# Opening of a fused attention and ReGLU kernel: scores of two tiles moved between the sums of the last image pair, half of that pair's last lines summed on TensorE

## Chip, cores, metric

One core of a Trainium2 chip (trn2). The metric is the device time of one execution in microseconds (us); lower is better. Times are compared only within the same rounds.

## The reference, cut to what matters

```
kv_pool = mean of kv over 4 x 4 pixels          # kv [4, 384, 32, 128] -> 768 keys per image
k = v   = kv_pool @ w_sr
a       = softmax(q @ k.T / sqrt(128))          # q [4, 12288, 128]
x       = a @ v
out     = (relu(x @ w_gate) * (x @ w_val)) @ w_out      # d_ff 1536; 49152 rows
```

## The kernel before

The rows of q are worked in 96 tiles of 512. The 768 keys of an image are six chunks of 128, loaded and pooled as three **pairs** of chunks (0, 1, 2). A pair arrives as four **lines** (the four pixel rows that are averaged), one transfer of 512 KB each. Its pooling is a sum of sixteen parts. In the opening most of that sum is done on TensorE: 128 x 128 transposes that accumulate in one PSUM bank turn and add at once. VectorE first adds two lines, which halves the number of transposes.

Only the opening, before the loop reaches its steady state, is touched by the change. Its helpers:

```python
def turn_add(b, pair, lines, first=False, final=False, chunks=(0, 1)):
    n = lines.shape[2]
    for h in chunks:
        for i in range(n):                                     # n = 4
            nc.tensor.matmul(kv_Ts[b, pair][:, h], lines[:, h, i], ident, is_transpose=True,
                start=(first and h == i == 0), stop=(final and i == n - 1), skip_group_check=True)
    if final and h == 1:
        kvT = work.tile([128, 2, 128], FP32, tag="kvT", bufs=2)
        nc.vector.tensor_copy(kvT, kv_Ts[b, pair])             # "the copy"
        kv_Ts[b, pair] = kvT

def project(b, pair):                                          # matmul with w_sr, then scaling on VectorE
    ...
def scores(k, jc):                                             # one 512-column matmul, one exponential
    s_ps = bank([128, T])
    nc.tensor.matmul(s_ps, kv16[:, k // NST, jc, 0:C], qT_of(k), start=True, stop=True)
    nc.scalar.activation(aTs[k][:, jc, :], s_ps, AF.Exp, scale=qk_scale)

def attend(k, pair):                                           # eight value matmuls
    for jc in (2 * pair, 2 * pair + 1):
        for half in range(2):
            values(k, jc, half)

def add_lines(pair, dh, engine, chunks=slice(0, 2)):           # line dh + line dh + 1
    ...
    engine.tensor_tensor(s2[:, chunks], line(pair, dh)[:, chunks], line(pair, dh + 1)[:, chunks], op=ALU.add)
    return s2
```

The part of the opening that the change touches:

```python
turn_open(0, 1)
turn_add(0, 1, add_lines(1, 0, nc.vector), first=True)
attend(0, 0)
for h in range(2):
    s2 = add_lines(1, 2, nc.vector, slice(h, h + 1))
    turn_add(0, 1, s2, final=True, chunks=[h])
attend(1, 0)
add_lines(2, 0, nc.gpsimd, slice(0, 1))
s2 = add_lines(2, 0, nc.vector, slice(1, 2))
...                                                            # weights and q loads issued from GpSimd
project(0, 1)
for k in range(GRP):                                           # GRP = 4
    for jc in range(2, 4):
        scores(k, jc)
    if k == 0:
        turn_values(0, 1)
    if k == 1:
        turn_open(0, 2)
        turn_add(0, 2, s2, first=True)
        for h in range(2):
            s2 = add_lines(2, 2, nc.vector, slice(h, h + 1))
            turn_add(0, 2, s2, final=True, chunks=[h])
    if k == 2:
        project(0, 2)
attend(0, 1)
attend(1, 1)
for jc in range(4, NJC):                                       # NJC = 6
    scores(0, jc)
turn_values(0, 2)
for jc in range(4, NJC):
    scores(1, jc)
attend(0, 2)
...                                                            # reciprocals, values kept, turned; scores of tiles 2, 3
```

The bank pool has eight PSUM banks. In the traces each engine's instructions start in the order written (below, for example, an addition of VectorE at 20.66 us that waited for a transfer, and behind it a scaling at 21.27).

The softmax here doesn't subtract the row's maximum and nothing guards it: scores larger than these inputs give would overflow.

## Time and profile before

| | before |
|---|---|
| time, median of the first 3 runs | 1048.71 us (1048.25 to 1049.2) |
| span of the profiled run | 1046.4 us |
| TensorE idle in its matmul records, 24 to 33 us | 1.29 us |
| TensorE waits, 43 to 1043 us | none |

The lines that carry the argument are shown in the prediction. Four moments, each the start of an instruction, are used throughout the rest:

- **a1**: VectorE starts to add lines 2 and 3 of pair 1, because the last of them has landed.
- **t0**: the first score matmul of pair 1 (tile 0) starts.
- **a2**: VectorE starts to add lines 2 and 3 of the last pair, because the last of them has landed.
- **V**: the first value projection, with which the loop begins.

In the order of time of the kernel before (start, length, engine, line of the program, operation, tiles, count, idle time just before and what ended it), a1, t0, a2 and V are these four:

```profile
17.42 1.29 DVE L343 TENSOR_TENSOR kv_s<-parts 128x512 f32<-128x512 f32 x2 [0.44 <-DMA parts<-in_kv_dram]
...
21.33 0.60 PE L185 MATMUL bank_ps<-qT,kv 128*128 128x512 f16 x2 [0.52 <-DVE kv L167]
...
24.00 1.29 DVE L343 TENSOR_TENSOR kv_s<-parts 128x512 f32<-128x512 f32 x2 [1.62 <-DMA parts<-in_kv_dram]
...
32.82 0.38 PE L234 MATMUL bank_ps<-xT,wv 128*128 128x512 f16 x1
```

Each of the two additions waited for a transfer. V lies 8.82 us behind a2.

### The profile page before, as it was taken

How to read it: one execution, taken by the hardware profiler on the slowest of the kernel's cores; microseconds unless marked ns; L12 is line 12 of the kernel's file. 1: busy time of each engine (PE TensorE's matmuls, PEld its weight loads, DVE VectorE, ACT ScalarE, POOL GpSimd, SP SyncE). 2: the span in 40 equal slices, each digit the busy share in tenths (PEclk: the TensorE clock that was granted, in tenths of full speed). 3: DMA queues.
4: the chain of work that ended last, by engine and by line, in shares of the span. 5: the costliest groups of instructions: out<-in, count | busy, mean ns of one | idle time of the engine just before them, and what ended most of it. 6: DMA issues, size and time to landing. Idle time of an engine off the chain costs nothing.

```text
span 1046.4 us, 25971 instructions
## 1 busy us (share of the span) xinstructions
PE 1036.4 (99%) x9980; PEld 691.1 (66%) x9980; DVE 913.8 (87%) x1680; ACT 908.5 (87%) x1741; POOL 107.6 (10%) x127
## 2 busy tenths in 40 slices
PE   7999999999999999999999999999999999999998
PEld 6566666666666666666666666666666666666665
DVE  3788889898888888898888888889988888888898
ACT  2988888888888888888888888888888888888887
POOL 2000045200000015500000003430000000000000
PEclk9999999999999999999999999999999999999999
DMA  8833256231322335523224134551331322212111
GB/s 302 119 81 69 70 191 162 57 87 32 84 54 62 76 122 140 154 62 72 54 64 87 31 87 132 147 152 40 78 65 53 72 63 55 67 32 67 32 47 47
DMA packets 125853, 90.75 MB, mean 87 GB/s; under 512 B 103328, under 2 KB 104224, under 8 KB 125728
## 3 DMA queue, kind: packets, MB, share of 16 engines
q1 hardware_dynamic: 120288, 75.85, 26.8%
q0 software_dynamic: 5440, 13.24, 7.7%
q8 instruction: 78, 1.28, 0.5%
q14 instruction: 47, 0.39, 0.1%
HBM read 52.76 MB, written 25.17 MB: 74 GB/s over the span
## 4 chain that ended last, share of the span: by engine, by line
PE 97%; DMA 2%; SPq 0%; DVE 0%; ACT 0%; issue 0%; DVEq 0%; ACTq 0%
PE bank_ps L255 25%; PE bank_ps L234 24%; PE bank_ps L245 24%; PE bank_ps L196 12%; PE bank_ps L185 12%; DMA parts<-in_kv_dram 1%; DMA q<-in_q_dram 1%; PE bank_ps L166 0%; PE bank_ps L154 0%; SPq L128 0%; ACT val L238 0%; PE bank_ps L174 0%; PE bank_ps L227 0%; DVE kv_s L343 0%; DVE rinv L204 0%
## 5 line engine op out<-in xcount | busy, mean ns | idle before, releaser
L248 DVE SCALAR_TENSOR_TENSOR hT<-bank_ps,val 128x512 f16<-128x512 f32 x1152 | 759.6, 686 | 100.9 <-ACT val L238 74.5
L238 ACT CAST val<-bank_ps 128x512 f16<-128x512 f32 x1152 | 677.8, 591 | 112.1 <-PE bank_ps L234 107.5
L255 PEld LDWEIGHTS <-hT 128*128 128x128 f16 x4608 | 351.4, 98 | 199.9 <-issue 0.4
L255 PE MATMUL bank_ps<-wo,hT 128*128 128x128 f16 x4608 | 443.2, 219 | 0.0
L234 PE MATMUL bank_ps<-xT,wv 128*128 128x512 f16 x1152 | 436.6, 379 | 0.1
L245 PE MATMUL bank_ps<-xT,wg 128*128 128x512 f16 x1152 | 435.7, 378 | 0.1
L186 ACT ACTIVATE aT<-bank_ps 128x512 f16<-128x512 f32 x576 | 346.3, 605 | 18.4 <-PE bank_ps L185 18.4
L196 PE MATMUL bank_ps<-kv,aT 128*128 128x129 f16 x2304 | 223.3, 219 | 0.0
L196 PEld LDWEIGHTS <-aT 128*128 128x128 f16 x2304 | 177.3, 98 | 68.4 <-issue 0.4
L185 PE MATMUL bank_ps<-qT,kv 128*128 128x512 f16 x576 | 216.4, 379 | 1.5 <-DVE kv L167 0.8
L245 PEld LDWEIGHTS <-wg 128*128 128x128 f16 x1152 | 111.5, 97 | 66.1 <-issue 1.0
L234 PEld LDWEIGHTS <-wv 128*128 128x128 f16 x1152 | 112.7, 98 | 0.4 <-issue 0.4
L212 DVE TENSOR_TENSOR x<-bank_ps,rinv 128x256 f16<-128x256 f32 x188 | 79.7, 424 | 6.7 <-DVE rinv L204 0.2
L78 POOL DMA_DIRECT2D q<-in_q_dram x23 | 12.5, 543 | 571.8 <-DMA qT<-q 571.5
L273 DVE TENSOR_SCALAR o_sb<-bank_ps 128x512 f32<-128x512 f32 (+1 forms) x95 | 64.0, 673 | 1.3 <-PE bank_ps L255 1.3
L137 POOL TENSOR_TENSOR s<-parts 128x512 f32<-128x512 f32 x36 | 45.3, 1270 | 162.7 <-DMA parts<-in_kv_dram 122.3
L185 PEld LDWEIGHTS <-kv 128*128 128x128 f16 x576 | 55.9, 98 | 2.4 <-DVE kv L167 1.4
L204 DVE RECIPROCAL rinv<-bank_ps 128x2 f32<-128x2 f32 x192 | 30.5, 159 | 1.2 <-PE bank_ps L196 1.2
L139 POOL TENSOR_TENSOR s<-s 128x512 f32<-128x512 f32 x18 | 22.8, 1268 | 1.4
L141 POOL TENSOR_TENSOR c<-s 128x256 f32<-128x256 f32 x18 | 13.0, 725 | 1.4
L161 DVE COPY kvT<-bank_ps 128x256 f32<-128x256 f32 x12 | 5.0, 415 | 7.2 <-PE bank_ps L154 7.2
L154 PE MATMUL bank_ps<-ident,kv_s 128*128 128x128 f32 x50 | 7.8, 275 | 1.6 <-DVE kv_s L343 1.6
(37 smaller groups left out, 83.3 us busy)
## 6 DMA issues: line engine op xcount, KB each, us to landing
parts<-in_kv_dram SPq DMA_DIRECT2D x48, 512.0 KB, 6.1
out_dram<-o_sb SPq DMA_DIRECT2D x95, 256.0 KB, 2.1
q<-in_q_dram POOLq DMA_DIRECT2D x23, 512.0 KB, 5.2
xT<-x SPq DMA_TRANSPOSE x94, 2.5
q<-in_q_dram SPq DMA_DIRECT2D x1, 768.0 KB, 7.9
wv<-in_moe_w_val_dram POOLq DMA_DIRECT2D x2, 192.0 KB, 4.6
wg<-in_moe_w_gate_dram POOLq DMA_DIRECT2D x2, 192.0 KB, 5.1
wo<-in_moe_w_out_dram POOLq DMA_DIRECT2D x1, 384.0 KB, 9.9
```

The lines of the kernel that those rows point to most:

```text
L137: eng.tensor_tensor(s2[:, i], parts[:, 2 * i, h], parts[:, 2 * i + 1, h], op=ALU.add)
L185: nc.tensor.matmul(s_ps, kv16[:, k // NST, jc, 0:C], qT_of(k), start=True, stop=True)
L186: nc.scalar.activation(aTs[k][:, jc, :], s_ps, AF.Exp, scale=qk_scale)
L196: nc.tensor.matmul(x_ps[:, i, :], aTs[k][:, jc, s * 128 : (s + 1) * 128], kv16[:, k // NST, jc, C : 2 * C + 1], start=(jc == 0 and i == 0) ...
L204: nc.vector.reciprocal(rinvs[k, half], x_banks[k, half][:, :, C : C + 1])
L212: nc.vector.tensor_tensor(x16s[k][:, 2 * half : 2 * half + 2, :], x_ps[:, :, 0:C], rinv.to_broadcast([128, 2, C]), op=ALU.mult,)
L234: nc.tensor.matmul(va_ps, wv16[:, fb * 128 : (fb + 1) * 128], xTs[k], start=True, stop=True)
L238: nc.scalar.copy(val, va_ps)
L245: nc.tensor.matmul(g_ps, wg16[:, fb * 128 : (fb + 1) * 128], xTs[k], start=True, stop=True)
L248: nc.vector.scalar_tensor_tensor(hTs[k][:, fb, :], g_ps, 0.0, vals.pop((k, fb)), op0=ALU.max, op1=ALU.mult)
L255: nc.tensor.matmul(o_ps, hTs[k][:, fb, s * 128 : (s + 1) * 128], wo16[:, fb, :], start=first, stop=(fb == NFB - 1), skip_group_check=True,)
L273: nc.vector.tensor_scalar(o_sb, o_ps, 1.0 / X_SCALE**2, None, op0=ALU.mult)
```

## The change

The intent: fill the time in which TensorE and ScalarE wait for the last pair's last line with the scores of tiles 2 and 3 for pair 1, and shorten the path from that line to the copy. For this, chunk 0 of lines 2 and 3 is turned straight from the landed lines (eight transposes) while VectorE adds chunk 1 alone (four transposes). The value matmuls of tile 1 for pair 1 also move, from in front of the last pair's first scores to behind them.

```diff
--- before.py
+++ after.py
@@ -382,36 +382,35 @@
     nc.gpsimd.dma_start(wo16, moe_w_out.rearrange("(fb f) c -> f fb c", f=128))
     q_load(2)
     project(0, 1)
-    for k in range(GRP):
-        for jc in range(2, 4):
+
+    def scores_of(k, pair):
+        for jc in (2 * pair, 2 * pair + 1):
             scores(k, jc)
-        if k == 0:
-            turn_values(0, 1)
-        if k == 1:
-            turn_open(0, 2)
-            turn_add(0, 2, s2, first=True)
-            for h in range(2):
-                s2 = add_lines(2, 2, nc.vector, slice(h, h + 1))
-                turn_add(0, 2, s2, final=True, chunks=[h])
-        if k == 2:
-            project(0, 2)
+
+    scores_of(0, 1)
+    turn_values(0, 1)
+    scores_of(1, 1)
+    turn_open(0, 2)
+    turn_add(0, 2, s2, first=True)
+    scores_of(2, 1)
+    turn_add(0, 2, line(2, 2), chunks=[0])
+    turn_add(0, 2, line(2, 3), chunks=[0], final=True)
+    turn_add(0, 2, add_lines(2, 2, nc.vector, slice(1, 2)), chunks=[1], final=True)
+    scores_of(3, 1)
+    project(0, 2)
     attend(0, 1)
+    scores_of(0, 2)
+    turn_values(0, 2)
+    scores_of(1, 2)
     attend(1, 1)
-    for jc in range(4, NJC):
-        scores(0, jc)
-    turn_values(0, 2)
-    for jc in range(4, NJC):
-        scores(1, jc)
     attend(0, 2)
     for half in range(2):
         keep_sums(0, half)
     for half in range(2):
         keep_values(0, half)
-    for jc in range(4, NJC):
-        scores(2, jc)
+    scores_of(2, 2)
     x_turn_pe(0)
-    for jc in range(4, NJC):
-        scores(3, jc)
+    scores_of(3, 2)
     attend(1, 2)
     for half in range(2):
         keep_sums(1, half)
```

## The prediction

> **What bounds the kernel now.** I write S(k,p) for the two score matmuls of query tile k with pooled-image pair p (pairs 0 to 2, so pair 1 is the second and pair 2 the last), E(k,p) for the two exponentials on ScalarE that follow, and A(k,p) for the eight value matmuls that use those. I read the page first, then the waits of TensorE by stage, then the chain of waits and the order of time over the opening.
>
> The page: busy shares, the slices, and the chain that ended last.
>
> ```profile
> PE 1036.4 (99%) x9980; PEld 691.1 (66%) x9980; DVE 913.8 (87%) x1680; ACT 908.5 (87%) x1741; POOL 107.6 (10%) x127
> PE   7999999999999999999999999999999999999998
> PE 97%; DMA 2%; SPq 0%; DVE 0%; ACT 0%; issue 0%; DVEq 0%; ACTq 0%
> ```
>
> The reader is to see one engine that never stops after the first slice. Asked for TensorE's waits from 43 to 1043 us, the profile lists none. Every slot of that stretch is filled by matmuls in program order, so whatever brings the start of that stretch forward by x us should bring the end forward by x, and nothing else in the change touches it. The whole question lies before 43 us. The busy time by stage (first column TensorE) shows how much room there is:
>
> ```profile
> 24.00:33.00 9.00, 7.71 (x69) 4.99 (x70) 4.33 (x13) 6.28 (x12) 2.13 (x4) 1.00 1.22 180
> 33.00:42.50 9.50, 8.96 (x74) 5.25 (x73) 7.54 (x18) 7.66 (x19) 0.53 (x1) 1.00 0.88 125
> ```
>
> TensorE is idle by these records for 1.29 us in the first stage and 0.54 us in the second. The chain of waits for that stage, in order of time (start, length, what):
>
> ```profile
> 12.22 11.65 DMA parts<-in_kv_dram
> ...
> 24.00 0.70 DVE kv_s L343
> ...
> 24.75 1.27 PE bank_ps L154 x8
> ...
> 26.04 0.44 DVE kvT L161
> ...
> 26.61 0.67 PE bank_ps L166 x2
> ...
> 27.71 0.91 PE bank_ps L196 x16
> ...
> 30.34 0.28 DVE rinv L204 x2
> 30.62 0.36 DVE x L212
> ```
>
> The last line of the last pair lands at 23.87. Until VectorE has added lines 2 and 3, TensorE has nothing to do, although S(2,1) needs only what has been there since 21.3. ScalarE waits with it. From the order of time:
>
> ```profile
> 22.62 1.03 PE L154 MATMUL bank_ps<-ident,kv_s 128*128 128x128 f32 x8
> 24.75 1.26 PE L154 MATMUL bank_ps<-ident,kv_s 128*128 128x128 f32 x8 [1.10 <-DVE kv_s L343]
> 25.84 0.59 PE L185 MATMUL bank_ps<-qT,kv 128*128 128x512 f16 x2
> 26.25 1.08 ACT L186 ACTIVATE aT<-bank_ps 128x512 f16<-128x512 f32 x2 [2.44 <-PE bank_ps L185]
> ```
>
> 1.10 us of TensorE and 2.44 us of ScalarE are lost in that one hole.
>
> **What the Trainium skill says.** "Perfetto Trace Analysis", § Identifying the Most-Contended Engine: a high matmul busy share does not say how near the engine is to its roofline. Here 99% against 66% for weight loads. I therefore rest on the empty list of waits and the in-order chain, not on the 99%. "VectorE: DVE Perf Modes", § The TRN2 errata: an fp32 addition of two tensors takes (N+151)/0.96 ns, so 691 ns for N=512. The trace agrees (0.69 us each, two in 1.29). "TensorE: Matmul & The Clock Gate", § Part 4: PE-mode transpose: some 275 ns in one kernel. The trace agrees in length (272 to 273), but what counts here is the spacing: eight in 1.03 us, so (1.03-0.27)/7 = 0.108 us. "PSUM — Partial Sum Buffer", § Specifications: 8 banks. In this stage four hold the running sums of tiles 0 and 1 and one the open transposes, so three are left for scores, and a score can wait for an exponential; the built program shows such waits.
>
> **The change part by part.** The order of instructions in the built program shows: S(2,1) before the sums of lines 2 and 3; chunk 0 of lines 2 and 3 as eight transposes straight from the landed lines, with four from a VectorE sum for chunk 1; S(3,1) before the projection; A(1,1) after S(1,2). Removed: one addition of 0.69 us. Added: four transposes, 4 x 0.108 = 0.43 us on TensorE. From the first value projection on, both programs have the same order, with waits that differ only in the first projection. The count of banks used is the same.
>
> I carry TensorE's clock through. The steps taken from the trace: 0.22 us per 512-column matmul, 0.057 per value matmul (16 in 0.91), exponential 0.41 after its score starts, one each 0.515, each ending after 0.61; transposed pair copy to projection 0.57 (26.04 to 26.61); projection to its scaling 0.71; scaling to score 0.49 (20.84 to 21.33); projection occupies TensorE 0.51.
>
> - The eight early transposes end issue at 22.62 + 8 x 0.108 = 23.49. S(2,1) starts there instead of at 25.84, since its banks were freed by exponentials of 22.27 and 22.78. TensorE is free at 23.92. E(2,1) starts at 23.90, no longer at 26.25.
> - Eight transposes of chunk 0, 23.92 to 24.79. Line 3 is there at 23.87; four of line 2 stand before it. Chunk 1's addition, 24.00 to 24.69, lies beside them. Its four transposes issue 24.79 to 25.22, the last ends at 25.11 + 0.27 = 25.39. The copy starts at 25.42, against 26.04: **0.62 us earlier**.
> - S(3,1) fills 25.22 to 25.66. Projection 25.42 + 0.57 = 25.99, scaling 26.70, A(0,1) from 26.50 to 26.96 beside it. S(0,2) at 26.70 + 0.49 = 27.19, against 28.46: **1.27 us earlier**, because before S(3,1), A(0,1) and A(1,1) all stood in front of it although its keys were ready (27.32 + 0.49 = 27.81).
> - Some is given back. S(0,2) 27.19 and 27.41, two transposes, S(1,2) first at 27.74. Its second waits for a bank until the exponential of 27.60 ends, 28.25. Then A(1,1), 8 x 0.057 = 0.46, 28.47 to 28.93. A(0,2) follows without a wait; before, its second half waited for an exponential until 30.04. Six of its eight are issued at 28.93 to 29.22, ending 29.43, so the reciprocal starts at 29.45, against 30.34: **0.89 us earlier**.
> - From there the chain is the old one. First turned values 31.03 - 0.89 = 30.14, S(3,2) 30.59, first value projection 32.82 - 0.89 = 31.93. ScalarE: its last four exponentials start at 29.8, 30.3, 31.0 and 31.5, the last ends at 32.1, before the first value cast at 32.34.
>
> Sum: **0.89 us**. Time 1048.71 - 0.89 = **1047.8 us**.
>
> **The rivals.**
> 1. **Only the sums count.** If the larger step at S(0,2) were wholly paid back by A(1,1) and the bank wait, the gain would be the 0.62 us of the earlier copy or less: 1048.1. For: between S(1,2)'s two halves TensorE has only three free banks. Against: 28.46 was set by order, and A(0,2)'s old wait disappears.
> 2. **A transfer anchors the start of the steady stage.** The next four query tiles are loaded and turned by transfers whose times do not move; the turn is done at 39.8 at the latest (the next load, which waits for it, starts at 39.81). They are first read at 42.33, afterwards 41.4, so 1.6 us are left. The output weights are issued at 24.52 and land 9.9 us later, 34.4, first used at 41.24. Neither binds. If one did, the gain would shrink to nothing: 1048.7.
> 3. **The coupled stage 33 to 42 takes the gain.** There VectorE and ScalarE wait in turns for each other (three ScalarE waits for reciprocals of 0.46 to 0.57). But both are fed by the value projections and should shift with them. If the shift let TensorE run ahead and wait longer at the end, the gain would be 0.3 to 0.6: 1048.2.
> 4. **Direct transposes are slower.** Those of pair 0, straight from lines, took 421 ns in the median, with weight loads of 231 against 140. If this came from the source and not from a TensorE just out of idleness, eight at 0.18 add 0.58 us to that step and eat the 0.62: 1048.4 or so. For the other reading: weight loads of the same identity were slow too.
>
> **Range and chances.** The three runs of before spread by 0.95 us, as much as the gain. The chain's uncertainty is some 0.4 each way, a median of few runs adds 0.4, and the landing at 23.87 can itself move by some tenths. So 1046.9 to 1048.9 for 8 in 10. 2% would be 21 us, and the opening before 43 us has 1.8 us of TensorE idle after 24 us in all: within 2% is all but certain, 0.99.
>
> **What would show it.** In the profile after: the 1.10 us hole at 24.75 gone and E(2,1) at about 23.9; the twelve transposes 23.9 to 25.4; the copy at 25.4; S(0,2) at 27.2; a bank wait of some 0.3 us in S(1,2); the first reciprocal at 29.45; the first value projection at 31.9; the first matmul with output weights near 40.35; and after 42 us no wait of TensorE, the same distance to the end. It would be wrong if the pair landed later for reasons of its own, if direct transposes were spaced at 0.18 us, or if TensorE began to wait in the stage from 33 to 42.

## The result, and the profile after

The changed kernel took 1047.75 us in the median of six runs (1047.64 to 1048.29); before took 1048.48 us in the six runs of the same rounds and the first look (1047.68 to 1049.20). Ratios in this document are the mean time of one kernel's runs over the mean of the other's runs of the same rounds, so they are not quite the ratio of the medians: here 0.9995, with a 95% interval of 0.9982 to 1.0007. The interval is wide against the effect, so most of the evidence below comes from moments inside the traces, which repeat to some hundredths of a us.

The page of the changed kernel, the lines that answer to those of before:

```profile
PE 1036.3 (99%) x9984; PEld 691.0 (66%) x9984; DVE 913.6 (87%) x1679; ACT 908.6 (87%) x1741; POOL 107.6 (10%) x127
PE   8999999999999999999999999999999999999998
PE 97%; DMA 1%; SPq 1%; DVE 1%; ACT 0%; issue 0%; DVEq 0%; ACTq 0%
```

Four matmuls more, one VectorE instruction less, as the diff says; the first slice went from 7 to 8 tenths. The opening in the order of time:

```profile
18.04 1.29 DVE L343 TENSOR_TENSOR kv_s<-parts 128x512 f32<-128x512 f32 x2 [1.09 <-DMA parts<-in_kv_dram]
...
21.84 0.60 PE L185 MATMUL bank_ps<-qT,kv 128*128 128x512 f16 x2 [0.52 <-DVE kv L167]
...
22.27 3.24 ACT L186 ACTIVATE aT<-bank_ps 128x512 f16<-128x512 f32 x6 [3.79 <-PE bank_ps L185]
...
24.00 0.59 PE L185 MATMUL bank_ps<-qT,kv 128*128 128x512 f16 x2
24.06 0.69 DVE L343 TENSOR_TENSOR kv_s<-parts 128x512 f32<-128x512 f32 x1 [1.18 <-DMA parts<-in_kv_dram]
...
24.43 1.04 PE L154 MATMUL bank_ps<-ident,parts 128*128 128x128 f32 x8
...
32.46 0.38 PE L234 MATMUL bank_ps<-xT,wv 128*128 128x512 f16 x1
```

The reader is to see two things. First, the hole is gone: TensorE goes from the two scores at 24.00 into the direct transposes at 24.43 without a wait, and ScalarE's six exponentials stand in one block. Second, this run did not start as the run of before did: a1 is 18.04 and not 17.42, t0 21.84 and not 21.33, while a2 hardly moved (24.06 against 24.00). Pair 1's last line landed 0.6 us later in that run, although the two kernels are the same up to there. Measured from its own t0, V comes after 10.62 us, against 11.49 before. Measured against the clock it comes only 0.36 us earlier, and the span is 0.3 us shorter.

The chain of waits says the same. Before it ran back from the loop to the last line's transfer. After it does not pass that line at all, but runs back through the work of pair 1 to pair 1's last line:

```profile
7.02 10.92 DMA parts<-in_kv_dram
...
18.04 0.70 DVE kv_s L343
...
24.59 1.33 PE bank_ps L154 x12
```

### The profile page after: what moved, and what is told of

Same layout as the page of the kernel before. It is cut to its first block, busy times and chain, and to the rows that moved or that the text cites. A ratio compares the mean times of both kernels' runs of the same rounds, so it can differ in the third digit from the quotient of the medians. Undisturbed runs are those within 1.5% of the kernel's fastest.

```text
span 1046.1 us, 25977 instructions
## 1 busy us (share of the span) xinstructions
PE 1036.3 (99%) x9984; PEld 691.0 (66%) x9984; DVE 913.6 (87%) x1679; ACT 908.6 (87%) x1741; POOL 107.6 (10%) x127
## 4 chain that ended last, share of the span: by engine, by line
PE 97%; DMA 1%; SPq 1%; DVE 1%; ACT 0%; issue 0%; DVEq 0%; ACTq 0%
PE bank_ps L255 25%; PE bank_ps L234 24%; PE bank_ps L245 24%; PE bank_ps L196 12%; PE bank_ps L185 12%; DMA parts<-in_kv_dram 1%; PE bank_ps L154 1%; PE bank_ps L166 1%; SPq L128 0%; ACT aT L186 0%; ACT x L210 0%; ACT val L238 0%; SPq L93 0%; PE bank_ps L174 0%; DVE hT L248 0%
## 5 line engine op out<-in xcount | busy, mean ns | idle before, releaser
L144 POOL TENSOR_TENSOR kv_s<-c 128x128 f32<-128x128 f32 x18 | 8.2, 454 | 1.4
```

## The experiments

The theory after this reading: the opening has **two starts that compete**. One is the last line's landing (a2), the other is the work of pair 1 in front of it (t0, which is a1 + 3.8: 3.91 in the profile of before, 3.80 in that of after). Before, V was set by a2 and came at a2 + 8.82. After, V is set by t0 and comes at t0 + 10.62. So the gain is (a2 + 8.82) - (t0 + 10.62): 0.87 us with the landings of the profile of before, 0.42 with those of the profile of after. The main rival is the simple reading of the change: a hole of 1.1 us was filled with scores, and that is the gain, wherever the landings fall. All kernels below gave correct results.

### Only the new order

Lines 2 and 3 of both chunks are again added on VectorE; the order of scores and values is the new one.

```diff
-    turn_add(0, 2, line(2, 2), chunks=[0])
-    turn_add(0, 2, line(2, 3), chunks=[0], final=True)
-    turn_add(0, 2, add_lines(2, 2, nc.vector, slice(1, 2)), chunks=[1], final=True)
+    for h in range(2):
+        s2 = add_lines(2, 2, nc.vector, slice(h, h + 1))
+        turn_add(0, 2, s2, final=True, chunks=[h])
```

> The new order of scores and values is kept, but both chunks of lines 2 and 3 are again added on VectorE. Let t0 be the start of the first score matmul of pair 1, a2 the start of VectorE's addition of the last pair's lines, V the first value projection. Before: V = a2 + 8.82 in its profile. After: V = t0 + 10.62 in its profile. Theory (last line's landing and the work of pair 1 are two competing starts, and the direct lines are worth more than the order): the copy of the turned pair comes at a2 + 2.04 as before, and V = the later of a2 + 8.56 and t0 + 10.62; so only 0.26 us earlier than before for the same a2. Rival (the gain comes from the scores pulled into the hole): V 0.5 to 0.9 earlier than a2 + 8.82.

a2 was 23.89. The copy and V, in the order of time of this kernel:

```profile
25.93 0.42 DVE L161 COPY kvT<-bank_ps 128x256 f32<-128x256 f32 x1 [0.75 <-PE bank_ps L154]
...
32.45 0.38 PE L234 MATMUL bank_ps<-xT,wv 128*128 128x512 f16 x1
```

The copy is at a2 + 2.04, V at a2 + 8.56, exactly as the theory had it: the new order as a whole is worth 0.26 us against the same landing, not 0.5 to 0.9. (Two parts are in it, the scores in the hole and the moved values of tile 1; the run "The values of tile 1 put back" parts them.) The time shows nothing (mean 1048.26, before 1048.13 in the same rounds, ratio 1.0001, 0.9988 to 1.0013).

### Only the lines on TensorE

The order of before, with the direct transposes of chunk 0.

```diff
-            for h in range(2):
-                s2 = add_lines(2, 2, nc.vector, slice(h, h + 1))
-                turn_add(0, 2, s2, final=True, chunks=[h])
+            turn_add(0, 2, line(2, 2), chunks=[0])
+            turn_add(0, 2, line(2, 3), chunks=[0], final=True)
+            turn_add(0, 2, add_lines(2, 2, nc.vector, slice(1, 2)), chunks=[1], final=True)
```

> The old order of scores and values, but chunk 0 of lines 2 and 3 straight on TensorE. Theory: copy at a2 + 1.38 when the landing is late, and V = the later of a2 + 8.16 and t0 + 10.44, so 0.66 us earlier than before for the same a2, and in some draws of the two landings even earlier than the full change. Rival (the gain comes from the scores pulled into the hole): V at a2 + 8.6 or later, no more than 0.2 us earlier than before. Time of the run 1047.8 against 1048.2 to 1048.5.

Measured, in the order of time of this kernel:

```profile
22.07 0.60 PE L185 MATMUL bank_ps<-qT,kv 128*128 128x512 f16 x2 [0.52 <-DVE kv L167]
...
32.52 0.38 PE L234 MATMUL bank_ps<-xT,wv 128*128 128x512 f16 x1
```

The landings were a1 = 18.26 and a2 = 23.75, so t0 was late and the last line early. V is t0 + 10.45; the theory gave 10.44. The rival's moment (a2 + 8.6 or later) is met too, with a2 + 8.77, because the last line came early; so this run supports the bound by t0 but does not tell the two readings apart. The full change would have had V at t0 + 10.62 = 32.69 in this draw: here a part of the change is better than the whole. The next run shows which part of the rest costs these 0.17 us. The worth of the direct lines for a late landing (0.66 us by the steps) was not reached in this draw; the run with the values cut in two, below, shows it at the copy. The mean was 1047.95, before 1048.13 in the same rounds (ratio 0.9997, 0.9984 to 1.0011).

### The values of tile 1 put back

```diff
     attend(0, 1)
+    attend(1, 1)
     scores_of(0, 2)
     turn_values(0, 2)
     scores_of(1, 2)
-    attend(1, 1)
```

> The full change, but the value matmuls of tile 1 for pair 1 stand again in front of the scores of tile 0 for the last pair. My prediction counted their move as part of the order's gain (the scores come 0.22 us earlier). Theory from the trace of after: the first score of the last pair comes 0.22 us later against the copy (1.99 in place of 1.76), but the reciprocal comes 1.88 after that score and not 2.28, so V is 0.17 us earlier than after for the same start: the later of t0 + 10.45 and a2 + 7.73. Rival (the move is a gain): V 0.2 us or more later than t0 + 10.62.

t0 was 21.93 and V 32.38, so V came at t0 + 10.45: 0.17 us earlier than with the full change, as the theory had it. The move of the eight value matmuls brings the last pair's scores forward by 0.22 us, but 0.46 us of values then stand between those scores and the first reciprocal, and only part of it fills a wait. This part of the change is a small loss. The scores themselves are neutral in such a draw: the run before, without them in the hole, had the same t0 + 10.45. (Mean 1047.81, before 1048.13, ratio 0.9997, 0.9984 to 1.0009.)

### Pair 1 treated in the same way

```diff
-    for h in range(2):
-        s2 = add_lines(1, 2, nc.vector, slice(h, h + 1))
-        turn_add(0, 1, s2, final=True, chunks=[h])
+    turn_add(0, 1, line(1, 2), chunks=[0])
+    turn_add(0, 1, line(1, 3), chunks=[0], final=True)
+    turn_add(0, 1, add_lines(1, 2, nc.vector, slice(1, 2)), chunks=[1], final=True)
```

> The full change, and chunk 0 of lines 2 and 3 of pair 1 also straight on TensorE. Let a1 be the start of VectorE's addition of lines 2 and 3 of pair 1. In before and after t0 = a1 + 3.91 and a1 + 3.80. Theory (after is bound by the work of pair 1): t0 = a1 + 3.14, and V = the later of t0 + 10.62 and a2 + 7.90, so earlier than after by up to 0.66 us, less where the last line lands late. Rival (after is bound by the last landing): V unchanged against a2, at the same a2 + 8.2 to 8.4 as in after.

Half a miss. a1 was 18.10, a2 23.20, V 32.36. V = t0 + 10.62 held to the hundredth (t0 21.74), and a2 + 8.2 to 8.4 (31.4 to 31.6) did not, so the kernel is bound by pair 1's work. But t0 was a1 + 3.64 and not 3.14. The larger part of these 0.50 us is the copy: it came at a1 + 1.72 and not 1.38 (0.34 us later), since value matmuls of tile 0 stood in front of the direct transposes. From the copy to t0 it took 1.92 us in place of 1.76, and VectorE's rows say why, in the order of time of this kernel:

```profile
20.66 0.69 DVE L343 TENSOR_TENSOR kv_s<-parts 128x512 f32<-128x512 f32 x1 [0.42 <-DMA parts<-in_kv_dram]
...
21.27 0.42 DVE L167 TENSOR_SCALAR kv<-bank_ps 128x256 f16<-128x256 f32 x1
```

The projection of pair 1 was ready earlier, but its scaling stood behind the addition of the last pair's lines 0 and 1 in VectorE's queue, and that addition waited for a transfer. A wait that had been hidden now cost some 0.16 us. (Mean 1048.02, before 1048.13, ratio 0.9999, 0.9986 to 1.0011.)

### The values of tile 1 cut in two

```diff
     attend(0, 1)
+    for half in range(2):
+        values(1, 2, half)
     scores_of(0, 2)
     turn_values(0, 2)
-    scores_of(1, 2)
-    attend(1, 1)
+    scores(1, 4)
+    for half in range(2):
+        values(1, 3, half)
+    scores(1, 5)
```

> The full change, but the value matmuls of tile 1 for pair 1 are cut in two: four in front of the first scores of the last pair, where TensorE waits 0.24 us for their keys in after, four between the two scores of tile 1, where it waits some 0.3 us for a bank. Theory (the moved values fill a wait only where they are cut to it): the reciprocal comes 1.88 us after the first score of the last pair in place of 2.28, and that score keeps its place 1.76 after the copy; V = the later of t0 + 10.23 and a2 + 7.51, 0.39 us earlier than after for the same start. Rival (ScalarE's exponentials are the next bound, no slack left): V less than 0.15 us earlier than t0 + 10.62.

In the order of time of this kernel (a2, the copy, V):

```profile
24.41 0.69 DVE L343 TENSOR_TENSOR kv_s<-parts 128x512 f32<-128x512 f32 x1 [1.78 <-DMA parts<-in_kv_dram]
...
25.85 0.42 DVE L161 COPY kvT<-bank_ps 128x256 f32<-128x256 f32 x1 [0.75 <-PE bank_ps L154]
...
31.99 0.38 PE L234 MATMUL bank_ps<-xT,wv 128*128 128x512 f16 x1
```

t0 was 21.59, a2 24.41, V 31.99: t0 + 10.40 and a2 + 7.58. The later of the two expected moments was a2 + 7.51 = 31.92, so the theory is off by 0.07; the copy came at a2 + 1.44 where the theory had 1.38. This is the one run with direct lines in which the last line landed late enough to bind. Against the copy of before at a2 + 2.04 the direct lines are worth 0.60 us here, near the 0.66 of the steps. The reciprocal at 29.50 came 1.89 after the last pair's first score at 27.61, as expected. ScalarE was not the next bound: against t0 + 10.62 = 32.21 the kernel is 0.22 earlier, limited here by a late landing. Mean 1047.54, before 1048.12 in the same rounds, ratio 0.9994 (0.9980 to 1.0008).

### The split, and both pairs, with VectorE's queue put in order

The edits of the last two runs, and these two:

```diff
-    attend(0, 0)
     turn_add(0, 1, line(1, 2), chunks=[0])
     turn_add(0, 1, line(1, 3), chunks=[0], final=True)
     turn_add(0, 1, add_lines(1, 2, nc.vector, slice(1, 2)), chunks=[1], final=True)
+    attend(0, 0)
     ...
-    s2 = add_lines(2, 0, nc.vector, slice(1, 2))
     ...
     project(0, 1)
+    s2 = add_lines(2, 0, nc.vector, slice(1, 2))
```

> As the split, and pair 1 is treated like the last pair: chunk 0 of its lines 2 and 3 straight on TensorE, with the value matmuls of tile 0 moved behind these, and VectorE's addition of the last pair's lines 0 and 1 moved behind the scaling of pair 1, since in the run on pair 1 alone VectorE stood there waiting for a later transfer. Theory: t0 = a1 + 3.17 (3.80 in after, 3.64 in the run on pair 1 alone); V = the later of t0 + 10.23 and a2 + 7.51, so for typical landings (a1 = 18.0, a2 = 23.9) 31.4, some 1.1 us earlier than after's 32.46, and now bound by both landings alike. Time near 1046.9. Rival (something else holds the opening, as the transfers' own pace or GpSimd's addition, 1.76 us after it waits for its line): V no earlier than 32.0.

a1 was 17.56, t0 20.88 (a1 + 3.32; 3.17 was expected, and value matmuls of tiles 0 and 1 stood in front of the projection), a2 23.63 and V 31.31. This is 1.15 us earlier than the profile of after and 1.51 earlier than that of before, and 1.14 earlier than the formula of before gives for this draw (a2 + 8.82 = 32.45). It is 0.17 us later than the theory's 31.14. Against its own t0 it is late by 0.20 (t0 + 10.43 in place of 10.23). Most of that is a collision of VectorE and GpSimd, in the order of time of this kernel:

```profile
20.17 1.26 POOL L343 TENSOR_TENSOR kv_s<-parts 128x512 f32<-128x512 f32 x1 [18.40 <-DMA parts<-in_kv_dram]
...
20.74 1.25 DVE L343 TENSOR_TENSOR kv_s<-parts 128x512 f32<-128x512 f32 x1
```

VectorE's addition takes 0.69 us in all other places and 1.25 here, ending 0.56 us after GpSimd's addition ends at 21.43. The Trainium skill, "SBUF — State Buffer", § SBUF: two separate sides, says that a VectorE instruction with two SBUF inputs and a GpSimd instruction that reads SBUF exclude each other for their whole length; this trace agrees, but for some 0.13 us: VectorE ended 0.56 us after GpSimd, less than its own 0.69. In the other order, as in before, VectorE's addition took its 0.69 us and GpSimd's, started 0.05 us behind it, took 1.76 us in place of the 1.26 here. The transposes that need the sum then started at t0 + 1.45 instead of t0 + 1.29.

The mean was 1047.43 against 1048.12 for before in the same rounds (medians 1047.51 and 1048.02; ratio 0.9993, 0.9981 to 1.0006). By its trace it beats both kernels. By its times it lies 0.69 us under before, which the interval does not make certain; "near 1046.9" was expected, and only the profiled run reached that (1046.94).

### Pair 1's work delayed on purpose, in both kernels

Both kernels get the same delay in front of t0. The landings stay where they are, so this makes the last line early in comparison.

```diff
     project(0, 1)
+    idle = bank([128, 128])
+    for _ in range(40):
+        nc.tensor.matmul(idle, ident16, ident16, start=True, stop=True)
```

> The full change, with 40 dummy matmuls of 128 columns (2.28 us) on TensorE in front of the first score of pair 1: t0 comes 1.60 us later, the landings stay. Theory (two competing starts): after is bound by t0, V = t0 + 10.62, so some 33.6 and the time 1.4 us longer than after. Compared with the same delay put into before it is slower by 0.2 to 0.6 us: the change is a loss where the last line lands early against the work of pair 1. Rival (the change gains 0.9 us wherever the landings fall): V 0.9 us earlier than with the delay in before.

> The kernel before with the same 40 dummy matmuls. Theory: with the line landed by the time that TensorE comes to it, the copy is at the later of t0 + 3.22 and a2 + 2.04, and V 6.78 after it, so the later of t0 + 10.00 and a2 + 8.82: some 33.0 to 33.3, only 0.2 to 0.7 us later than before. Rival (as in the other delayed run): V 0.9 us later than with the delay in the full change.

The order of time, first with the delay in the changed kernel, then with the delay in the kernel before (t0 and V of each):

```profile
23.25 0.59 PE L185 MATMUL bank_ps<-qT,kv 128*128 128x512 f16 x2
...
33.86 0.38 PE L234 MATMUL bank_ps<-xT,wv 128*128 128x512 f16 x1
```

```profile
23.21 0.59 PE L185 MATMUL bank_ps<-qT,kv 128*128 128x512 f16 x2
...
33.21 0.38 PE L234 MATMUL bank_ps<-xT,wv 128*128 128x512 f16 x1
```

The changed kernel has V at t0 + 10.61, the kernel before at t0 + 10.00. With the same delay the changed kernel is **slower by 0.65 us** in the trace, a little more than the 0.2 to 0.6 expected. The times of the same rounds agree: means 1049.48 and 1048.75, every run of the first but one above every run of the second (the exception is 1048.92 against 1049.12). The rival, which expected 0.9 us of gain here too, falls. The steps account for it: where the last line is early, the four additional transposes (4 x 0.108 = 0.43 us) buy nothing, the moved values cost 0.17 us, and the moved scores cost in front of the copy the 0.43 us that they save behind it. Sum 0.60, seen 0.61 from t0.

### Both kernels once more

> The kernel before, unchanged: a second draw of the landings, and a control of the timing (its ratio to itself should be 1.0000 within the interval). Theory: V = the later of a2 + 8.82 and t0 + 10.00, whatever a1, t0 and a2 come out at; a1 between 17.4 and 18.3, a2 between 23.6 and 24.4 as in the runs so far. Rival (the steps are not fixed, only this profile's): V off by more than 0.1.

> The changed kernel, unchanged: a second draw. Theory: V = the later of t0 + 10.62 and a2 + 7.96 (the copy came at a2 + 1.44 in the run with the split, 6.52 before V). In the same rounds as the kernel before again its mean should be 0.3 to 0.6 us lower, since the starts seen so far (t0 = a1 + 3.8 with a1 near 17.9, a2 near 23.95) give 32.77 for before and 32.3 for after on average, not the 0.89 that my prediction took from one profile.

New draws, and the formulas held. Before: a1 17.87, a2 24.51, V 33.33 = a2 + 8.82. After: a1 17.95, t0 21.75, a2 23.38, V 32.37 = t0 + 10.62. In the same rounds the means were 1048.61 (before, as a kernel under test), 1048.52 (before, nine runs) and 1047.99 (after). One expectation missed: a2 of before was to lie between 23.6 and 24.4. Before against itself is 1.0001, after against before 0.9995 (0.9982 to 1.0009), 0.53 us.

### The last pair landing later on purpose

One more transfer of 512 KB, into a tile that nothing reads, between the lines of pair 1 and those of the last pair.

```diff
+    late = const.tile([128, 2, r, C], FP32)
     for pair in range(1, NJC // 2):
+        if pair == 2:
+            nc.sync.dma_start(late..., kv[B - 1, 0 : 2 * HC]...[0])
         kv_load(0, pair)
```

> The kernel before with one more transfer of 512 KB (into a tile that nothing reads) between the lines of pair 1 and those of the last pair: at the 400 GB/s of the opening the last line lands 1.3 us later, pair 1's lines stay. Theory: V = a2 + 8.82, so V near 34.1. Rival: none for this kernel alone; it is the partner of the next.

> The full change with the same extra transfer. Theory: now the landing binds the changed kernel too, V = a2 + 7.96, so 0.86 us earlier than before for the same a2, and no more than that however late the line. Rival 1 (the change hides the landing altogether): V stays at t0 + 10.62, near 32.3. Rival 2 (the gain is the scores in the hole, so it grows with the hole): V more than 1.2 us earlier than a2 + 8.82.

This pair did not test what it was built for. All four lines of the last pair came later, and VectorE's addition of its lines 0 and 1 stands in front of the scaling of pair 1, so t0 moved too (22.92 in the kernel before, 23.23 in the changed one, with a2 24.80 and 25.31). The formulas still held: before V 33.61 (a2 + 8.82 = 33.62; 34.1 was expected, from a later landing), after 33.85 (t0 + 10.62). V is later in the changed kernel, but so were both of its starts; in either draw the formulas give the changed kernel a gain (0.08 and 0.28 us, estimates). Rival 1's offset, t0 + 10.62, held as well, and only its "near 32.3" failed, because t0 moved; this pair says nothing against it. The run with the values cut in two does: there V was set by the landing (a2 + 7.58). Whether the changed kernel's gain stops at 0.86 us for a late line was not shown; the extra transfer ought to have gone between lines 1 and 2. Times: means 1049.79 (before) and 1050.28 (changed), with runs up to 1051.84.

### All draws in one table

V by the trace, and the formula that each kernel has by the steps above; "rest" is the span minus V.

| kernel | a1 | t0 | a2 | V | formula | rest (span known to 0.1) |
|---|---|---|---|---|---|---|
| before | 17.42 | 21.33 | 24.00 | 32.82 | a2 + 8.82 (taken from here) | 1013.58 |
| before again | 17.87 | 21.68 | 24.51 | 33.33 | 33.33 | 1013.57 |
| after | 18.04 | 21.84 | 24.06 | 32.46 | t0 + 10.62 (taken from here) | 1013.64 |
| after again | 17.95 | 21.75 | 23.38 | 32.37 | 32.37 | 1013.63 |
| only the order | 17.65 | 21.45 | 23.89 | 32.45 | 32.45 | 1013.65 |
| only the lines | 18.26 | 22.07 | 23.75 | 32.52 | 32.51 | 1013.58 |
| values back | 18.13 | 21.93 | 24.09 | 32.38 | 32.38 | 1013.62 |
| pair 1 too | 18.10 | 21.74 | 23.20 | 32.36 | 32.36 | 1013.64 |
| split | 17.79 | 21.59 | 24.41 | 31.99 | 31.92 | 1013.61 |
| both pairs | 17.56 | 20.88 | 23.63 | 31.31 | 31.14 | 1013.59 |
| delay, after | 17.89 | 23.25 | 24.20 | 33.86 | 33.87 | 1013.64 |
| delay, before | 17.86 | 23.21 | 24.16 | 33.21 | 33.21 | 1013.59 |
| late, before | 18.02 | 22.92 | 24.80 | 33.61 | 33.62 | 1013.59 |
| late, after | 18.32 | 23.23 | 25.31 | 33.85 | 33.85 | 1013.55 |

(In the two delayed runs VectorE's addition waited for its turn and not for the line, so their a2 is no landing.) The last column moves by 0.1 us over fourteen traces, which is no more than the spans are known to, while V moves by 2.5: what the opening gains or loses reaches the end one for one.

## Why the prediction was right, point by point

**The time and the range.** 1047.8 was predicted, 1047.75 measured. Neither says much: the range (1046.9 to 1048.9) also holds the 1048.48 of before, and part of the agreement with 1047.8 is luck, as the point on the mis-sized term shows.

**Pass-through.** "Whatever brings the start of that stretch forward by x us should bring the end forward by x": shown by the constant rest. No transfer anchors the steady stage (rival 2), and the coupled stage from 33 to 42 us takes nothing (rival 3).

**The steps on TensorE.** Measured from t0, each was right to some hundredths. Predicted and measured offsets: first moved score 2.16 and 2.16, direct transposes 2.59 and 2.59, copy 4.09 and 4.10, projection 4.66 and 4.67, first score of the last pair 5.86 and 5.86, first reciprocal 8.12 and 8.14, V 10.60 and 10.62. The expected wait for a bank between the last pair's two scores of tile 1 is there too (0.31 us, for "some 0.3").

**Rival 1, only the sums count.** It falls by the steps: from the copy to V before took 6.78 us (26.04 to 32.82) and after 6.52 (25.94 to 32.46), so 0.26 us came in addition to the earlier copy.

**Rival 4, slow direct transposes.** It falls: eight straight from the lines took 1.04 us, against 1.03 from a sum. And in the profile of before again the transposes of pair 0, from the lines too, took 273 ns in the median where the prediction had read 421, so the source was not the reason.

**What was worth what.** The prediction did not say which part gained. The order alone is 0.26 us for a late landing (shown; 0.43 for the two scores less 0.17 for the values), and the direct lines are 0.66 by the steps (0.60 at the copy, in the one run that reached it). "Some is given back" was right and understated: the move of tile 1's values is a net loss of 0.17 us.

**The term that was mis-sized.** The prediction carried the profile's t0 and landing into the changed kernel as if they were constants, and allowed only that the landing "can itself move by some tenths". It named a pair that "landed later for reasons of its own" as a sign of being wrong, but not that pair 1's landing sets t0. The sum of 0.89 us is a2 - t0 - 1.80 with that one draw (2.67 - 1.80 = 0.87, by the measured offsets). And that draw was the best case: a still later line would bind the changed kernel too, so the formulas cap the gain at 0.86 (by the offset a2 + 7.96, an estimate: copy at a2 + 1.44 from the run with the values cut in two, 6.52 from there to V). Over the ten profiles with undisturbed transfers, a1 runs from 17.42 to 18.26 and a2 from 23.20 to 24.51. Putting each draw into the formulas (t0 = a1 + 3.80 except where before's profile has its own, the gain held at that cap for late landings, and before's other bound of t0 + 10.00 kept) gives gains from -0.5 to +0.86, three of them below zero, and a mean of 0.37 us, an estimate. What decides is the distance from a1 to a2, which was 5.10 to 6.64 us in these profiles (6.58 in the one that the prediction used). The two timed comparisons gave 0.57 and 0.53 us by their means. So the size of the change is best put at some 0.4 to 0.6 us in place of 0.89. No interval makes that certain: the ratio's interval reaches from 1.9 us faster to 0.7 slower, so the medians' difference of 0.73, and the median of after at the predicted number, prove no more.

**What stays open.** Why the landings move is not shown. In before's trace the bulk of the last pair had arrived by 22.0 us, and from 22 to 23 only five packets with 0.02 MB in all came in (busy share 0.06, which is one of the core's 16 transfer engines), although the line was not complete until 23.87; a single lagging transfer engine would look like this, but no run was made on it. The draws also come from different kernels and chips. The changed kernel's own gain for a very late line is open too.

## What to carry to other kernels

When a wait is filled, look for the start that stands directly behind it: closing a hole of 1.1 us may gain only the distance to the next bound, and if both starts hang on transfers, that distance can change sign from run to run (by the formulas in three draws of ten; shown with the delay, 0.65 us slower). Additional work that an in-order engine does for free in a hole is a cost whenever the hole isn't there, and moved work is free only where it is cut to the size of the wait that it fills. Where an effect is smaller than the spread of times, measure moments in the trace from their own trigger (here t0 or a2) and check that the rest of the span is constant.

## What the Trainium skill lacked or had wrong

- "TensorE: Matmul & The Clock Gate", § Part 4: PE-mode transpose gives one transpose's length (some 275 ns in one kernel, in a sentence on bf16; the last pair's fp32 transposes took 272 to 273 ns here), but not the start-to-start spacing of fp32 transposes, on which the steps of this opening rest: eight in 1.03 us, 0.108 us apart.
- No page that I read gives the spread of one transfer's landing from run to run. Ten profiles of eight kernels with the same twelve loads had the last line of pair 1 ready at 17.42 to 18.26 us and that of the last pair at 23.20 to 24.51 us.
- "Perfetto Trace Analysis", § Optimization Strategy says to find a gap and the semaphore that ended it. It lacks the next step, the bound that stands behind the gap: here a hole of 1.10 us was closed, and the means of two timed comparisons differ by 0.53 and 0.57 us.
- "VectorE: DVE Perf Modes", § The TRN2 errata gives the length of an fp32 addition (691 ns at 512 elements; 0.69 us in the runs) without the case of GpSimd holding SBUF, where the same addition took 1.25 us. The SBUF page has the rule.
